# The opening of an attention and feed-forward kernel: softmax of the first batch in three groups of sets, x fetched ahead of the weights, three units opened together

## The chip, the cores and the metric

The kernel runs on one core of a Trainium2 chip. The metric is the device time of one execution in microseconds. The profile shows one execution on that core, with five instruction streams: PE (TensorE, with PEld for its weight loads), DVE (VectorE), ACT (ScalarE), POOL (GpSimd) and SP (SyncE, which here only issues DMAs).

## The reference

An attention block with inducing points is followed by a SwiGLU feed-forward block. There are 4 batches of 12416 tokens with 128 channels, 32 inducing points, and 1536 hidden channels.

```python
def mab(q, kv):
    s = scale * (q @ kv.transpose(0, 2, 1))
    s = s - s.max(-1, keepdims=True)
    a = np.exp(s)
    a /= a.sum(-1, keepdims=True) + 1e-09
    return a @ kv
h = mab(I, x)            # 32 inducing points attend to all tokens
x = mab(x, h)            # each token attends to the 32 rows of h
...
xn = x / rms * rms_g     # rms over the channels of a token
g = xn @ w_gate
silu = g * (1.0 / (1.0 + np.exp(-g)))
val = xn @ w_val
return (silu * val @ w_out).astype(np.float32)
```

The first softmax runs over all 12416 tokens of a batch, so no sum of it can be scaled before its last token has been seen. The weights of the feed-forward arrive as float64 and are turned to fp32 on the chip.

## The kernel before, in words

**Tiling.** A batch is cut into seven sets of tokens (`per`: five of 16 tiles of 128 tokens, one of 15, one of 2). A tile of x is turned to channels first by a PE transpose, `turn_x` (L313), four to a PSUM bank, and copied out by ACT (L316). `scores1` (L322, L326) multiplies a set with the inducing points, four groups of 32 rows side by side in one bank, and takes the maximum of each row as it copies the scores to SBUF. `max1`, `max2`, `max3` (L331 to L346) join the maxima of all sets: a reduction on DVE, a PE transpose, a reduction over the four groups and a scaling on DVE (`row`, `row4`), a PE matmul that turns the result back, and a copy of it to SBUF, the bias (`nbias`). `exp1_of` (L355) takes the exponential of one or two sets on ACT and sums its rows; `turn_e` (L364) transposes a set's exponentials in 32x32 blocks on DVE; `sum_h` (L378) multiplies them with the tokens on PE, with all seven sets in one PSUM bank. `fold_l` (L387, L389) adds up the row sums and takes the reciprocal, `divide` (L393) scales the sum, and `turn_h` (L398, L400) gives `hT`, the 32 rows of h with channels first.

From `hT` follow the second scores of set 0 (`scores2`, L322 and L424), the row maximum (L428, L432), the exponential (`exp2`, L439), and the steps of `seam`: a transpose, a product with the gram matrix of h for the rms (`square`, L499), row sums (L510), a power of -1/2 on POOL (`root`, L516), the scaling (`apply`, L520), a transpose and a split into an upper and a lower half (L524 to L533). `spread` (L555, L558) makes the first unit's moving operand out of these; `gather` (L545) makes those of later units by four DMAs.

**Weights.** Each weight matrix has three chunks (i, c): gate, value and output (i = 0, 1, 2), each for 512 hidden channels (c = 0, 1, 2). A chunk takes the steps `power`, `power_number`, `upper`, `upper_number`, `sign`, `lower` (L249 to L279): four on DVE, two on ACT (or on DVE where the code says so), the last product on POOL. Gate and value chunks are then multiplied with h (`stack_of` on PE and ACT, L467 and L468; `stack_low` on DVE, L472), since g = a (h w).

**Feed-forward units.** A unit is 512 tokens; a batch has 25, and each has 12 slots j, one for each 128 hidden channels. A slot is a gate matmul (L677), a silu on ACT (L685), a value matmul (L688), a product u on DVE (L694), and later the product with the output weights (L613), either plain in fp32 (two passes, 0.86 us) or as a three-part product of the kind of L633, L635 and L613, whose parts ACT, DVE and POOL prepare (L659 to L669). `acc` collects the unit's output.

**What sets the order.** No scheduler reorders: the code's order is the order on each engine's queue. The opening, up to the first slot, is written out by hand. From there a plan (`schedule`) puts the remaining weight steps, second scores and next batch's attention at given slots, and a rehearsal with costs by engine (`rehearse`, `decide`) settles which products are three-part ones and when each is issued. The slots of the first two units of batch 0 are sorted by weight chunk, so that the first eight slots need chunk 0 only. Calls of `warm` put matmuls with no use into PE's queue. [...] five in `ps_gv` (turns, scores, gate, value, stackings), two in `ps_acc`, one in `ps_u`.

**Queues.** All loads are issued on SP in the order: sets 0 to 3 of x, chunk (0,0), sets 4, 5 and 6 (four DMAs), then chunks (1,0), (2,0), (0,1) and (1,1); the two small loads (inducing points, gamma column) are on ACT's queue.

## Time and profile before

| | |
|---|---|
| time, median of 3 runs | 1623.82 us (1623.35 to 1623.96) |
| profiled run | 1623.49 us, span 1621.7 us |
| first turn of x on PE | 8.17 us |
| last pass of the first scores on DVE starts | 27.54 us |
| first exponential on ACT | 29.85 us |
| copy of hT on DVE | 39.45 us, 0.29 long |
| power of -1/2 on POOL | 48.29 us, 3.29 long |
| first gate matmul | 55.48 us |
| DMA share, 8 to 27 us | 0.93 |

A row of the timeline has the start, the duration, the engine, the line, the operation, the tile written, the tile read, their shapes, and in brackets how long the engine had been idle and what ended that. The chain of waits lists, in order of time, the pieces of work that the end depended on one after another. In the table of stretches each engine's column is its busy time within the stretch, and the last three columns are the granted PE clock, the share of the DMA engines that was busy, and GB/s.

### The profile page before, as it was taken

To read this page: it belongs to the slowest core of one execution; us is meant where nothing else is said; L and a number is where in the kernel's file an instruction comes from. 1 tells how busy PE (TensorE), PEld (TensorE's weight loads), DVE (VectorE), ACT (ScalarE), POOL (GpSimd) and SP (SyncE) were. 2 spreads that over 40 slices of the span, in tenths; PEclk is the share of its full clock that TensorE was granted. 3 is DMA by queue.
4 is the path that set the end of the run, shared out by engine and by line. 5 is a ranking of instruction groups with operands and counts; after the bars stand their busy time and mean duration, and the time that the engine had idled before them with its cause. 6 is when DMAs were issued, how large, how long until landed. Compare 5 with 4: busy or idle time off the path is not lost.

```text
span 1621.7 us, 25435 instructions
## 1 busy us (share of the span) xinstructions
PE 1604.3 (99%) x7085; PEld 1085.6 (67%) x7085; DVE 1444.6 (89%) x2504; ACT 1238.3 (76%) x2285; POOL 1217.7 (75%) x979
## 2 busy tenths in 40 slices
PE   8999999999999999999999999999999999999998
PEld 6546666756676666766677666676667777777776
DVE  4879988999899998899899998789989999999997
ACT  4567877767887778776778777877778888878886
POOL 1358885878588886688678888587858878878876
PEclk9999999999999999999999999999999999999999
DMA  7455624444353141634445323353221122111221
GB/s 262 91 72 85 112 43 97 88 97 69 60 94 59 36 95 29 133 76 81 69 67 83 55 54 68 63 125 79 46 38 29 31 39 40 35 35 36 40 38 26
DMA packets 389181, 112.52 MB, mean 69 GB/s; under 512 B 365072, under 2 KB 369712, under 8 KB 386480
## 3 DMA queue, kind: packets, MB, share of 16 engines
q1 hardware_dynamic: 388304, 110.82, 34.8%
q8 instruction: 56, 0.92, 0.3%
q14 instruction: 85, 0.70, 0.2%
q10 hardware_dynamic: 736, 0.08, 0.0%
HBM read 53.95 MB, written 27.00 MB: 50 GB/s over the span
## 4 chain that ended last, share of the span: by engine, by line
PE 94%; DVE 1%; ACT 1%; issue 1%; POOL 0%; DVEq 0%; ACTq 0%
PE acc L613 35%; PE gv L677 18%; PE gv L688 16%; PE u L635 10%; PE u L633 10%; PE gv L322 3%; PE gv L499 1%; PE gv L378 1%; DVE gv L694 1%; ACT silu L685 1%; PE gv L453 0%; DVE xn L660 0%; PE gv L467 0%; DVE o L621 0%; POOL xn L279 0%
## 5 line engine op out<-in xcount | busy, mean ns | idle before, releaser
L669 POOL TENSOR_TENSOR xn<-xn,xn 128x512 fp32r<-128x512 f32 (+2 forms) x705 | 870.9, 1255 | 268.6 <-DVE xn L660 156.8
L685 ACT ACTIVATE silu<-gv 128x512 f32<-128x512 f32 (+2 forms) x1186 | 689.7, 586 | 258.4 <-PE gv L677 231.8
L688 PE MATMUL gv<-a,sv 128*128 128x512 f32 (+2 forms) x1188 | 636.1, 536 | 0.8 <-ACT silu L685 0.8
L613 PE MATMUL acc<-u,wo 128*128 128x512 f32 (+1 forms) x990 | 490.8, 581 | 0.0
L677 PE MATMUL gv<-a,sg 128*128 128x512 f32 (+2 forms) x1188 | 486.7, 410 | 1.5 <-ACT silu L685 0.8
L694 DVE TENSOR_TENSOR u<-silu,gv 128x512 f32<-128x512 f32 (+2 forms) x621 | 407.7, 663 | 51.7 <-PE gv L688 32.3
L694 DVE TENSOR_TENSOR gv<-silu,gv 128x512 f32<-128x512 f32 (+2 forms) x565 | 376.0, 668 | 66.1 <-PE gv L688 49.0
L660 DVE SCALAR_TENSOR_TENSOR xn<-xn,gv 128x512 fp32r<-128x512 f32 (+2 forms) x566 | 371.3, 656 | 9.5 <-ACT xn L659 5.9
L659 ACT ACTIVATE xn<-gv 128x512 fp32r<-128x512 f32 (+2 forms) x566 | 330.4, 584 | 43.1 <-DVE gv L694 30.9
L677 PEld LDWEIGHTS gv<-a,sg 128*128 128x128 f32 x1188 | 223.8, 188 | 189.4 <-ACT silu L685 40.2
L688 PEld LDWEIGHTS gv<-a,sv 128*128 128x128 f32 x1188 | 223.6, 188 | 139.6 <-issue 46.3
L613 PE MATMUL acc<-xn,more 128*128 128x512 f32 (+2 forms) x705 | 273.6, 388 | 3.0 <-DVE o L621 2.6
L633 PE MATMUL u<-xn,xn 128*128 128x512 f32 (+2 forms) x705 | 272.4, 386 | 0.0
L613 PEld LDWEIGHTS acc<-u,wo 128*128 128x128 f32 x990 | 184.9, 188 | 46.7 <-issue 9.1
L664 POOL TENSOR_TENSOR xn<-u,xn 128x512 fp32r<-128x512 f32 (+2 forms) x139 | 178.6, 1285 | 41.6 <-ACT xn L663 41.6
L635 PE MATMUL u<-xn,xn 128*128 128x512 f32 (+2 forms) x414 | 160.1, 387 | 0.0
L613 PEld LDWEIGHTS acc<-xn,more 128*128 128x128 f32 x705 | 132.4, 188 | 33.5 <-POOL xn L669 5.7
L633 PEld LDWEIGHTS u<-xn,xn 128*128 128x128 f32 x705 | 132.6, 188 | 28.6 <-issue 5.5
L663 ACT ACTIVATE xn<-u 128x512 fp32r<-128x512 f32 (+2 forms) x139 | 87.4, 629 | 36.6 <-DVE u L694 32.4
L635 PE MATMUL u<-xn,more 128*128 128x512 f32 (+2 forms) x291 | 112.5, 387 | 0.0
L516 POOL TENSOR_TENSOR rs<-ms,mhalf 128x16 f32<-128x16 f32 (+2 forms) x28 | 75.9, 2709 | 18.1 <-DVE ms L511 17.1
L635 PEld LDWEIGHTS u<-xn,xn 128*128 128x128 f32 x414 | 77.7, 188 | 17.5 <-DVE gv L694 0.2
(151 smaller groups left out, 1096.9 us busy)
## 6 DMA issues: line engine op xcount, KB each, us to landing
out_dram<-o SPq DMA_DIRECT2D x320, 64.0 KB, 2.0
xT<-in_x_dram SPq DMA_DIRECT2D x60, 256.0 KB, 5.4
xn<-in_x_dram SPq DMA_DIRECT2D x60, 256.0 KB, 5.0
a<-hi SPq DMA_DIRECT2D x156, 64.0 KB, 2.0
a<-lo SPq DMA_DIRECT2D x156, 64.0 KB, 2.0
xn<-in_x_dram SPq DMA_DIRECT2D x5, 1024.0 KB, 10.6
xn<-w SPq DMA_DIRECT2D x18, 256.0 KB, 3.6
out_dram<-o SPq DMA_DIRECT2D x64, 60.0 KB, 2.0
```

What stands on the lines that cost most here:

```text
L613: nc.tensor.matmul(acc[:, 0:T], lhsT, rhs, start=st["left"] == NJ, stop=st["left"] == 1)
L633: nc.tensor.matmul(ups[:, 0:T], weight_of(0, j), hi, start=st["k"] == nk, stop=False)
L635: nc.tensor.matmul(ups[:, 0:T], weight_of(1, j), lo, start=False, stop=not st["k"])
L659: nc.scalar.activation(hi, v, AF.Copy, scale=(1.0 - 2.0 ** -13) * 2.0 ** -12)
L660: nc.vector.scalar_tensor_tensor(out=lo, in0=hi.bitcast(F32), scalar=-4096.0, in1=v, op0=ALU.mult, op1=ALU.add)
L663: nc.scalar.activation(d, v, AF.Copy, scale=1.0 - 2.0 ** -13)
L664: nc.gpsimd.tensor_tensor(out=lo, in0=v, in1=d.bitcast(F32), op=ALU.subtract)
L669: nc.gpsimd.tensor_tensor(out=d, in0=hi.bitcast(F32), in1=lo.bitcast(F32), op=ALU.subtract)
L677: nc.tensor.matmul(g[:, 0:T], sg[:, ts(j, P)], a[:, 0:T], start=True, stop=True)
L685: nc.scalar.activation(sl[:, 0:T], g[:, 0:T], AF.Silu)
L688: nc.tensor.matmul(v[:, 0:T], sv[:, ts(j, P)], a[:, 0:T], start=True, stop=True)
L694: nc.vector.tensor_tensor(out=t[:, 0:T], in0=sl[:, 0:T], in1=v[:, 0:T], op=ALU.mult)
```

## The change

It touches batch 0 only, apart from parameters that leave the other batches as they were.

- **Loads.** Set 6 of x comes first, as four DMAs on ACT's queue. Sets 0 to 5 follow on SP, with chunk (0,0) behind set 3, and set 5 in two DMAs (tiles 0 to 7, and the rest). The other four chunks follow behind set 5.
- **Softmax.** The sets are put in the groups 0 to 2, 3 to 4 and 5 to 6. Each group has a maximum of its own (`max1` to `max3` run three times), one exponential over its whole width and a PSUM bank of its own for its sum. `least` takes the smallest of the three biases, `shares` the exponentials of the differences, by which the row sums are weighted before `fold_l`; `divide` adds the three sums, each with its share and the common reciprocal, by one scaling and two fused multiply-adds.
- **Order of the opening.** Turns, scores, maxima, exponentials and sums of the groups are interleaved by hand. Two of the four copies of set 5 go to DVE. The calls of `warm` between the scores and the sums are gone. Chunk (0,0) is rounded between `max2` and `max3` of group 0 and behind that group's exponential; (1,0) around the end of the sums with its two number steps on ACT; (2,0) after the first exponential of the second softmax; (0,1) after `spread`.
- **First units.** Three units (`OPEN`) are opened together in place of two: the first 36 slots are sorted by chunk, so that the first 12 need chunk 0 only. The third unit's `acc` takes a bank of `ps_gv`. The plan puts chunks (1,1), (2,1), (2,2), (0,2), (1,2) at slots 2, 5, 8, 12, 16 and the stackings at 4, 8, 18, 22; the fourth unit's `gather` comes at slot j = 8 of the third.

```diff
+    GROUPS = (range(0, 3), range(3, 5), range(5, NS))
+    OPEN = 3
...
-                nc.sync.dma_start(out=t[ts(q, m), 0:n, :], in_=of(xrows, b, s)[q])
+                (nc.sync if b else nc.scalar).dma_start(out=t[ts(q, m), 0:n, :], in_=of(xrows, b, s)[q])
...
-            nc.sync.dma_start(out=t[:], in_=d)
+            for part in (slice(0, 8), slice(8, n)) if s == full - 1 else (slice(0, n),):
+                nc.sync.dma_start(out=t[:, part, :], in_=d[:, part, :])
...
-                nc.scalar.copy(out=dst, in_=src)
+                if k % 2 and s == full - 1:
+                    nc.vector.tensor_copy(out=dst, in_=src)
+                else:
+                    nc.scalar.copy(out=dst, in_=src)
...
+        def least():
+            st["least"] = small.tile([P, 1], F32, name="mx")
+            nc.vector.tensor_reduce(out=st["least"][:], in_=st["nb"][:], axis=AX.X, op=ALU.min)
+
+        def shares():
+
+            G, least = len(st["parts"]), st["least"]
+            share = st["share"] = small.tile([P, G], F32, name="rl")
+            nc.scalar.activation(share[:], st["nb"][:], AF.Exp, bias=least[:], scale=-1.0)
+            ls = st["ls"][:, 0:G]
+            nc.vector.tensor_tensor(out=ls, in0=ls, in1=share[:], op=ALU.mult)
+            nc.vector.reduce_sum(out=st["hl"][:, C:C + 1], in_=ls, axis=AX.X)
...
+                nc.vector.scalar_tensor_tensor(out=hn, in0=ps, scalar=share[:, g:g + 1], in1=hn, op0=ALU.mult, op1=ALU.add)
...
-        acc = ps_acc.tile([P, 512], F32, name="acc")
+        acc = bank() if not b and u == OPEN - 1 else ps_acc.tile([P, 512], F32, name="acc")
...
+    turn_x(0, *range(R))
+    f["scores1"](0)
+    turn_x(1, *range(R))
+    turn_x(2, *range(R))
+    f["scores1"](1)
+    f["scores1"](2)
+    f["max1"](0)
+    turn_x(3, *range(R))
+    f["max2"]()
+    parts(0, 0, nc.vector)
+    f["max3"](0)
+    f["exp1_of"](0, 3, 0)
+    f["scores1"](3)
+    join(0, 0)
+    f["turn_e"](0)
+    turn_x(4, *range(R))
+    f["turn_e"](1)
+    f["scores1"](4)
+    f["max1"](1)
+    turn_x(NS - 1, 0)
+    turn_x(5, 0, 1)
+    f["max2"]()
+    f["turn_e"](2)
+    f["scores1"](NS - 1)
+    f["max3"](1)
+    turn_x(5, 2, 3)
+    f["exp1_of"](3, 5, 1)
+    f["sum_h"](0)
+    f["scores1"](5)
+    f["max1"](2)
+    f["sum_h"](1)
+    f["turn_e"](3)
+    f["max2"]()
+    f["sum_h"](2)
+    f["turn_e"](4)
+    f["max3"](2)
+    f["exp1_of"](5, NS, 2)
+    f["least"]()
+    f["sum_h"](3)
+    f["sum_h"](4)
     one = weight[1, 0]
-    f["max1"]()
     one["power"]()
+    f["turn_e"](5)
+    f["turn_e"](6)
+    f["shares"]()
+    f["fold_l"]()
+    f["sum_h"](5)
+    f["sum_h"](6)
     one["upper"]()
+    one["power_number"]()
+    one["upper_number"]()
+    for g in range(len(GROUPS) - 1):
+        f["divide"](g)
+    one["sign"]()
+    f["divide"](len(GROUPS) - 1)
     f["turn_h"]()
...
-            for k, one in ((1, (2, 1)), (5, (0, 2)), (8, (1, 2)), (11, (2, 2))):
+            for k, one in ((2, (1, 1)), (5, (2, 1)), (8, (2, 2)), (12, (0, 2)), (16, (1, 2))):
...
-            for k, *one in ((2, 0, 1), (4, 1, 1), (11, 0, 2), (13, 1, 2)):
+            for k, *one in ((4, 0, 1), (8, 1, 1), (18, 0, 2), (22, 1, 2)):
...
-            order[:2 * NJ] = sorted(order[:2 * NJ], key=lambda one: (one[1] // R, one))
+            order[:OPEN * NJ] = sorted(order[:OPEN * NJ], key=lambda one: (one[1] // R, one))
```

## The prediction

> **What bounds the kernel now.** I read the page first: busy shares, then the chain that ended last.
>
> ```profile
> span 1621.7 us, 25435 instructions
> PE 1604.3 (99%) x7085; PEld 1085.6 (67%) x7085; DVE 1444.6 (89%) x2504; ACT 1238.3 (76%) x2285; POOL 1217.7 (75%) x979
> ...
> PE 94%; DVE 1%; ACT 1%; issue 1%; POOL 0%; DVEq 0%; ACTq 0%
> ```
>
> TensorE sets the end once the feed-forward units flow. The change leaves those units alone except the first three, so it can act only on the time before the first gate matmul, on the first 36 slots, and on the amount of TensorE work. The second view is the busy time by stretch (PE, PEld, DVE, ACT, POOL, clock, DMA share, GB/s).
>
> ```profile
> 8.00:27.00 19.00, 17.55 (x158) 12.24 (x158) 6.61 (x18) 12.30 (x25) 0.00 (x0) 1.00 0.93 369
> 27.00:40.00 13.00, 11.46 (x235) 9.48 (x237) 10.45 (x31) 5.06 (x10) 2.55 (x2) 1.00 0.41 124
> 40.00:55.50 15.50, 13.79 (x97) 10.70 (x89) 13.27 (x23) 7.10 (x14) 5.08 (x3) 1.00 0.14 41
> 55.50:62.40 6.90, 6.45 (x19) 3.44 (x20) 5.69 (x10) 4.28 (x8) 2.24 (x3) 1.00 0.60 163
> ```
>
> From 8 to 27 us TensorE (turns and scores of x) and the DMA are both nearly full and VectorE is idle two thirds of the time; from 27 to 40 VectorE is the full one. Of the opening's timeline these rows set prices:
>
> ```profile
> 23.70 0.42 DVE L249 TENSOR_SCALAR we<-sc 128x512 int32<-128x512 int32 x1
> 24.16 0.43 DVE L256 TENSOR_SCALAR we<-we 128x512 int32<-128x512 int32 x1
> 24.62 0.43 DVE L233 TENSOR_SCALAR we<-we 128x512 int32<-128x512 int32 x1
> 24.96 0.42 DVE L262 TENSOR_SCALAR o<-sc 128x512 int32<-128x512 int32 x1
> 25.41 0.43 DVE L233 TENSOR_SCALAR o<-o 128x512 f32<-128x512 int32 x1
> ...
> 29.65 0.16 DVE L346 COPY nbias<-gv 128x1 f32<-128x1 f32 x1 [0.20 <-PE gv L343]
> ...
> 29.85 0.72 ACT L355 ACTIVATE sc<-sc,nbias 128x512 f32<-128x512 f32 x1 [3.98 <-DVE nbias L346]
> 30.57 1.13 ACT L355 ACTIVATE sc<-sc,nbias 128x1024 f32<-128x1024 f32 x1
> ```
>
> The five instructions on weight chunk (0,0) hold VectorE 2.06 us (23.70 to 25.76). ScalarE waits 3.98 us for the bias of the one softmax.
>
> [...] L249 takes 0.80 at 27.88, while L279 runs on GpSimd, and 0.42 otherwise. [...] 0.69 for L326 from PSUM, 0.43 for the cast L532 from SBUF. [...] warm-up matmuls fill its waits; 20 cold ones at the start took 4.63 us, 16 warm ones at 29.55 took 2.05.
>
> **The change part by part.**
>
> *Loads.* Four issues for set 6 (0.31 to 0.42 each) leave SP and come on ScalarE ahead of its table load (1.68, 1.28 us), which then ends near 4.7; ScalarE's first copy starts at 8.80: hidden. In the built program chunk (0,0) waits in SP's queue for the gamma column (issue 1.21 plus 8.8 to landing: 10.0), with set 4 behind it; sets 2 and 3 keep the DMA full until 14.8, so nothing is lost. Set 4 landed at 18.5 (3.41+15.1), set 5 at 22.1 (4.50+17.6). The walk below wants them at 21.4 and 27.2, so the split of set 5 buys nothing either.
>
> *Groups.* I walk the new order with durations from before. Rates: a set's turns on PE 1.84, its copies on ACT 4x0.50, its scores 0.95, the scores pass on DVE 0.62 plus about 0.08, a transposed exponential 0.64, a set's sum 0.87. (Walked so, the scores of before end at 26.7; the last score matmuls of the trace end at 26.76.) Sets 0 to 2: scores of set 2 leave PE at 17.4, DVE has the group's maximum at 18.5, PE turns it behind set 3's turns at 19.3, row and row4 (0.27, 0.21) end at 20.15. Now the order puts the five (0,0) instructions ahead of the bias copy: +2.06, bias at 22.3. Behind that copy stand DVE's later passes, and ScalarE's exponential with all copies of set 4. The exponential over 1536 columns has no row; 0.72 and 1.13 give 0.41 per 512, so 1.54 (bounds 1.4 and 1.7). It ends at 23.9, set 4's copies at 25.9. PE, out of banks and inputs, stands from 23.2 to 26.0; set 4's scores end at 26.9. Group 1's maximum needs the DVE pass (27.8), a turn, one PSUM copy (0.6; bounds 0.43 and 0.72), row and row4: 29.4; bias 30.2. Set 5's second half is turned from 29.7, copied by 31.15, scored behind a sum from 31.3 to 32.2; its pass ends at 33.1, the third maximum at 33.3. Between 33.3 and 37.2 DVE does four transposes (0.64, two of them ahead of steps of the maximum), row, row4, bias (35.2), waits for the last exponential (36.06), two short transposes, and the new product and sum of the shares (0.15 each). Fold 0.42, reciprocal 0.17, upper 0.41, the scaling of shares 0.15, two of the three divides (0.35; the fused one bounded by 0.29 and 0.45): 39.2. Then the sign step, 0.6, stands ahead of the last divide: 40.15. Turn 0.49, copy 0.29: **hT at 41.0, against 39.74** (39.45+0.29). That is +1.3, bounds +0.5 and +2.1. The wins are real: in before 12.0 us pass from the last scores pass (27.76) to hT, in after 7.9. But the last scores come 5.3 later. The removed warm-ups (15) filled waits only: 0.
>
> *From hT to the first gate matmul* (55.48): scores, two-step maximum, exponential, gram, root (3.29 on GpSimd), apply, split, spread: 15.74 in before, each step waiting for the last. The order around it loses chunk (0,1) and half of (1,1) and gains (1,0)'s last step and all of (2,0). These fit where before had theirs, mostly under the root: 0.
>
> *First slots.* ScalarE now has two (0,1) steps (0.63, 0.60) between the spread's copy and the first silu: silu starts 0.65 later. From 55.48 to the gram matmul at 108.87 PE did 68 gate and value matmuls (0.2325), 28 products and 4 weight stackings (0.859), scores (5.24), one three-part product (0.70): 49.2 of 53.4, so 4.15 idle. After holds the same list but 29 products and no three-part one: 49.4. Of the idle time, 1.2 comes before the second stacking. With one stacking fewer ahead I get 1.05 including the late silu: -0.2. Some 0.5 lies at the wait for GpSimd's (1,2):
>
> ```profile
> 73.93 0.15 issue
> 74.08 1.35 POOL xn L279
> 75.43 0.04 issue
> 75.47 1.12 PE gv L467 x2
> ```
>
> (PE works until 75.0 meanwhile.) With chunks 1 and 2 needed at slots 12 and 24, not 8 and 16, it goes: -0.5. Against it, VectorE has a chunk and a half more to round (2.2 a chunk, 3.3 in all) in 36 slots; it was busy 24.0 of 31 from 78 to 109, so it holds. The third accumulator takes one of the five banks that gate, value, stacking and scores share, in slots 8 to 35: no row; between 0 and a wait of 0.15 in each of 28 slots, 4.2; I take +0.5.
>
> *Three-part products.* Two fewer in the built program (565 for 567 at 512 columns): 2x(0.859-0.70) = +0.3.
>
> **Sum:** +1.3-0.2-0.5+0.5+0.3 = +1.4 on a span of 1621.7, from a run of 1623.49; the three timed runs lie at 1623.35 to 1623.96. 1623.8+1.4 = **1625.2**.
>
> **Rivals.** *The clock drops.* PE's gap of 2.8 us ahead of set 4's scores [...] no warm-up fills it. For: nothing else is queued on PE; a GpSimd or exponential longer than priced widens it. Against: [...] the turns run at 0.112 each through 5.4 us at 11.9, so they keep the clock. [...] then scores (+0.95), 17 turns (+1.9) and a sum (+0.87) on the chain double: 3.7, of which I count 3.3 behind overlaps with VectorE: 1628.5, slower. *The lost bank decides.* 4.2 in place of 0.5: 1628.9; for it, a stacking bank is held about 3 us (PE, ACT cast, VectorE); against it, two slots' banks suffice on average. *The opening hides its steps and the ramp gains.* If VectorE is never the bound (bias and sign steps wait for nothing), hT comes at 39.0 or so (-2.0 to my walk), and three units remove 2.5 more of the 4.15 idle: 1620.6. For: less weight work per slot at first; against: VectorE's order is written out. *The change does not do what it says:* set 4 late behind the gamma wait. It needs 2.9 us of lateness; then the walk shifts by the rest; inside the ranges.
>
> **How the numbers follow.** Measurement tells 0.2% (3.2 us) from no change. Forecast 0.55 (own range 1622.8 to 1627.0), clock 0.15, bank 0.10, faster 0.20. The range reaches to the rivals: 1620.4 to 1628.7. Faster takes three quarters of the last rival, 0.15; slower most of the first two, 0.22; within 0.63.
>
> **What would show it.** First exponential near 22.4 and set 4's scores near 26 (right) or near 20.8 and 24 (faster rival); hT's copy near 40.7; first gate matmul near 56.8; turns at 0.23 each after 26 (clock); gate and value matmuls waiting for DVE or ACT in slots 8 to 35 (bank). Wrong altogether if the first gate matmul comes before 55.5.

## The result, and the profile after

The changed kernel takes **1635.93 us** (median of 4 runs, 1635.13 to 1636.19), the kernel before 1623.67 (4 runs, 1623.35 to 1623.96): a ratio of 1.0075, 95% interval 1.0057 to 1.0092. It is slower by 12.3 us where 1.4 were forecast, and lies outside the forecast range of 1620.4 to 1628.7. The page of after, its span, busy shares and the chain that ended last:

```profile
span 1633.2 us, 25381 instructions
...
PE 1606.0 (98%) x7059; PEld 1083.1 (66%) x7059; DVE 1447.8 (89%) x2512; ACT 1240.0 (76%) x2284; POOL 1218.5 (75%) x979
...
PE 93%; DVE 3%; ACT 2%; issue 1%; POOL 1%; DMA 0%; SPq 0%; DVEq 0%; POOLq 0%; ACTq 0%
```

TensorE still sets the end, with more of the chain on VectorE (3%, 1% in before) and ScalarE (2%, 1% in before). The busy time by stretch (PE, PEld, DVE, ACT, POOL, clock, DMA share, GB/s) tells where; the first two stretches are those shown of before, the third ends at the first gate matmul:

```profile
8.00:27.00 19.00, 14.98 (x120) 9.37 (x119) 8.09 (x22) 11.59 (x22) 1.27 (x1) 0.97 0.99 380
27.00:40.00 13.00, 11.47 (x235) 9.02 (x233) 8.49 (x31) 4.96 (x10) 0.00 (x0) 0.92 0.12 37
40.00:59.11 19.11, 15.19 (x98) 11.93 (x99) 14.57 (x25) 6.08 (x13) 5.95 (x4) 0.93 0.25 76
```

The clock column reads 0.97, 0.92 and 0.93 where before had 1.00 throughout: TensorE ran slower for part of each stretch. VectorE, the full engine from 27 to 40 in before (10.45 of 13), has 8.49.

**One offset has to be taken out first.** TensorE's first turn of x starts at 8.17 us in the run of before and at 7.22 in that of after, because the warm-up matmuls ahead of it come 0.21 us apart at first and 0.11 later, and the turn to the faster pace comes at 7.4 us in before and at 5.2 in after. So the same 33 matmuls, which start at 1.36 us in both, take 6.81 us and 5.86, and TensorE does not stand between them and the first turn. That is no part of the change. The opening of before ends (hT's copy) 31.57, 31.58, 31.57 and 31.58 us after its own first turn in all four runs here that have it, though the first turn itself lies anywhere from 7.11 to 8.17. So hT is counted from the first turn in what follows. With that, the loss falls into four stretches. "The gram matmul" is here the second one on TensorE (`square`, L499 in before and L530 in after); in every kernel of this document it comes behind 34 slots. A stretch ends with the end of hT's copy or the start of the matmul named:

| stretch | before | after | difference | forecast |
|---|---|---|---|---|
| first turn to hT | 31.57 | 34.47 | +2.9 | +1.3 |
| hT to the first gate matmul | 15.74 | 17.42 | +1.7 | 0 |
| first gate matmul to the gram matmul | 53.23 | 59.31 | +6.1 | −0.2 |
| gram matmul to the end | 1513.0 | 1514.8 | +1.8 | +0.3 |

They sum to +12.5; the two spans differ by 0.95 less, which is the earlier first turn. Half of the loss lies in these 34 slots. The same slots, split in three, in before (first fence) and in after (second):

```profile
55.48:74.00 18.52, 18.07 (x54) 9.97 (x55) 16.89 (x29) 12.07 (x22) 4.90 (x5) 1.00 0.76 152
74.00:90.00 16.00, 15.77 (x62) 7.02 (x61) 13.69 (x22) 10.60 (x19) 10.78 (x8) 1.00 0.55 79
90.00:108.71 18.71, 18.20 (x65) 8.51 (x64) 14.21 (x23) 13.11 (x20) 4.94 (x5) 1.00 0.41 60
```

```profile
59.11:78.00 18.89, 17.33 (x52) 9.13 (x51) 15.85 (x26) 11.64 (x22) 3.89 (x3) 0.98 0.65 132
78.00:99.00 21.00, 17.90 (x66) 7.40 (x65) 18.36 (x29) 12.27 (x23) 10.00 (x8) 1.00 0.34 64
99.00:118.42 19.42, 18.96 (x65) 8.82 (x64) 12.86 (x21) 13.30 (x20) 5.66 (x6) 1.00 0.43 67
```

The middle stretch carries it: TensorE stands 3.1 of 21.0 us, against 0.2 of 16.0. VectorE is busy 18.4 of 21.0 there, and 12.9 of 19.4 after it. What TensorE's matmuls waited for in these slots, in after (us in total, times, longest):

```profile
PE gv L708 <- DVE sg L503: 1.3, 1, 1.3
PE gv L644 <- DVE sv L503: 1.1, 1, 1.1
PE gv L330 <- ACT silu L716: 1.1, 1, 1.1
```

All three are waits for a bank: L503 is the last step of a stacking, which gives its bank back, and L716 is the silu that reads a gate matmul out of one. The second is the third unit's first product (`gv<-u,wo` at 76.01 us), whose sums move into a bank of `ps_gv`. Before has no wait above 0.5 us there. The question for the experiments was whether the bank is missing or the engines that give it back are late, and why.

### The profile page after: what moved, and what is told of

The parts are those of the page before. It is cut to its first block, busy times and chain, and to the rows that moved or that the text cites. A ratio compares the mean times of both kernels' runs of the same rounds, so it can differ in the third digit from the quotient of the medians.

```text
span 1633.2 us, 25381 instructions
## 1 busy us (share of the span) xinstructions
PE 1606.0 (98%) x7059; PEld 1083.1 (66%) x7059; DVE 1447.8 (89%) x2512; ACT 1240.0 (76%) x2284; POOL 1218.5 (75%) x979
## 4 chain that ended last, share of the span: by engine, by line
PE 93%; DVE 3%; ACT 2%; issue 1%; POOL 1%; DMA 0%; SPq 0%; DVEq 0%; POOLq 0%; ACTq 0%
PE acc L644 34%; PE gv L708 17%; PE gv L719 16%; PE u L666 10%; PE u L664 9%; PE gv L330 3%; PE gv L530 1%; PE gv L401 1%; ACT silu L716 1%; DVE gv L725 1%; ACT xT L324 0%; PE acc L186 0%; PE gv L318 0%; PE gv L484 0%; DVE u L725 0%
## 5 line engine op out<-in xcount | busy, mean ns | idle before, releaser
L700 POOL TENSOR_TENSOR xn<-xn,xn 128x512 fp32r<-128x512 f32 (+1 forms) x703 | 869.1, 1256 | 265.3 <-DVE xn L691 145.2
L716 ACT ACTIVATE silu<-gv 128x512 f32<-128x512 f32 (+2 forms) x1186 | 690.7, 587 | 255.9 <-PE gv L708 230.4
L644 PE MATMUL acc<-u,wo 128*128 128x512 f32 (+2 forms) x972 | 481.9, 580 | 0.0
L644 PE MATMUL acc<-xn,more 128*128 128x512 f32 (+1 forms) x702 | 272.5, 388 | 3.0 <-DVE o L652 2.7
L664 PE MATMUL u<-xn,xn 128*128 128x512 f32 (+1 forms) x703 | 271.6, 386 | 0.0
L695 POOL TENSOR_TENSOR xn<-u,xn 128x512 fp32r<-128x512 f32 (+1 forms) x141 | 181.5, 1287 | 42.5 <-ACT xn L694 42.5
L644 PEld LDWEIGHTS acc<-u,wo 128*128 128x128 f32 x972 | 181.4, 188 | 45.6 <-issue 8.4
L666 PE MATMUL u<-xn,xn 128*128 128x512 f32 (+2 forms) x412 | 159.3, 387 | 0.0
L694 ACT ACTIVATE xn<-u 128x512 fp32r<-128x512 f32 (+1 forms) x141 | 88.8, 630 | 37.7 <-DVE u L725 32.8
```

What stands on the lines that cost most here:

```text
L644: nc.tensor.matmul(acc[:, 0:T], lhsT, rhs, start=st["left"] == NJ, stop=st["left"] == 1)
L664: nc.tensor.matmul(ups[:, 0:T], weight_of(0, j), hi, start=st["k"] == nk, stop=False)
L666: nc.tensor.matmul(ups[:, 0:T], weight_of(1, j), lo, start=False, stop=not st["k"])
L694: nc.scalar.activation(d, v, AF.Copy, scale=1.0 - 2.0 ** -13)
L695: nc.gpsimd.tensor_tensor(out=lo, in0=v, in1=d.bitcast(F32), op=ALU.subtract)
L700: nc.gpsimd.tensor_tensor(out=d, in0=hi.bitcast(F32), in1=lo.bitcast(F32), op=ALU.subtract)
```

## The experiments

The table gives the median time of each run, its ratio to the kernel before on the same chip with the interval, and the four stretches of its own profile. Five runs whose first slots are those of after (after, x4, x9, y1, z1) give 59.24 to 59.43 for the third stretch, so in that column a difference of 0.2 says nothing.

| run | us | ratio, 95% | turn to hT | to gate | to gram | to end |
|---|---|---|---|---|---|---|
| x1_three_old_opening | 1624.89 | 1.0012 [1.0005, 1.0018] | 31.58 | 15.73 | 53.56 | 1514.6 |
| x2_two_new_opening | 1630.57 | 1.0045 [1.0030, 1.0060] | 34.06 | 17.41 | 56.39 | 1513.3 |
| x3_bank_back | 1632.42 | 1.0058 [1.0043, 1.0073] | 35.52 | 16.86 | 57.66 | 1514.2 |
| x4_warm | 1633.99 | 1.0066 [1.0049, 1.0083] | 34.03 | 17.43 | 59.39 | 1514.5 |
| x5_bank_held | 1624.68 | 1.0010 [1.0003, 1.0017] | 31.57 | 15.74 | 54.41 | 1513.6 |
| x6_fetch | 1633.22 | 1.0064 [1.0049, 1.0079] | 34.59 | 16.85 | 58.11 | 1514.9 |
| x7_lower | 1636.72 | 1.0082 [1.0067, 1.0098] | 35.52 | 15.81 | 60.97 | 1514.3 |
| x8_weights_early | 1632.28 | 1.0057 [1.0042, 1.0072] | 34.59 | 16.86 | 56.11 | 1515.0 |
| x9_warm_short | 1633.61 | 1.0064 [1.0049, 1.0079] | 32.97 | 16.86 | 59.43 | 1514.5 |
| y1_opening | 1633.92 | 1.0065 [1.0048, 1.0081] | 33.53 | 17.53 | 59.24 | 1514.6 |
| y2_two | 1627.93 | 1.0029 [1.0018, 1.0040] | 33.53 | 15.92 | 56.50 | 1513.3 |
| y3_three | 1626.45 | 1.0021 [1.0013, 1.0029] | 31.90 | 15.92 | 54.50 | 1514.0 |
| z4_bank_early | 1630.51 | 1.0044 [1.0029, 1.0059] | 32.97 | 16.86 | 54.79 | 1514.9 |
| z1_gather | 1635.33 | 1.0073 [1.0057, 1.0090] | 34.09 | 17.41 | 59.25 | 1514.5 |
| z2_three_bank_gather | 1623.14 | 1.0001 [0.9992, 1.0009] | 31.58 | 15.75 | 52.62 | 1514.1 |
| z3_opening | 1625.19 | 1.0013 [1.0006, 1.0020] | 31.32 | 15.92 | 54.50 | 1514.2 |

### Opening or first slots: each with the other's partner

**x1**, the kernel before with the three units alone:

```
+    OPEN = 3
-        acc = ps_acc.tile([P, 512], F32, name="acc")
+        acc = bank() if not b and u == OPEN - 1 else ps_acc.tile([P, 512], F32, name="acc")
-            order[:2 * NJ] = sorted(order[:2 * NJ],
+            order[:OPEN * NJ] = sorted(order[:OPEN * NJ],
...
```

> The kernel before, with its own opening and its own order of rounding and stacking, and only its first three units opened together, the third adding up in one of the five banks of gate and value. In the changed kernel the stretch from first gate matmul to gram matmul takes 59.3 us, in the kernel before 53.2. Bank theory (the third unit's sums hold a bank that gate, value, stacking and scores need): most of these 6 us come with the three units, so that stretch takes 57 to 60 us here, and the time is 1628 to 1631 us. Weight theory (the rounding that the new opening leaves to the first slots, and the late raw chunk, hold VectorE): the stretch takes 53 to 55 us, and the time is 1623.5 to 1625.5. Either way the first gate matmul stays at 55.5 us.

53.6 us, 1624.9: the weight theory's numbers. Three units and a lost bank by themselves cost 0.3 us in the first slots (and 1.6 behind the gram matmul).

**x2**, the changed kernel with two units:

```
-    OPEN = 3
+    OPEN = 2
-            for k, one in ((2, (1, 1)), (5, (2, 1)), (8, (2, 2)), (12, (0, 2)), (16, (1, 2))):
+            for k, one in ((1, (1, 1)), (3, (2, 1)), (6, (0, 2)), (9, (1, 2)), (12, (2, 2))):
-            for k, *one in ((4, 0, 1), (8, 1, 1), (18, 0, 2), (22, 1, 2)):
+            for k, *one in ((3, 0, 1), (6, 1, 1), (11, 0, 2), (14, 1, 2)):
...
```

> The changed kernel with its opening, but two units opened together, both adding up in their own banks; the weights that the opening leaves over are rounded in the order of the kernel before, each some slots later. The opening should give 3.6 us over the kernel before, as in the changed kernel (first gate matmul at 59.1 us). Bank theory: the stretch to the gram matmul takes 53 to 55 us, the time is 1627 to 1629. Weight theory: this stretch takes 57 to 60 us here too, the time is 1630 to 1634.

Between the two: 56.4 us, 1630.6. Without any lost bank the new opening still costs the first slots 3.2 us. It leaves one chunk more to them (22 rounding steps on VectorE where before has 18), and the four stackings wait 2.4 us in all for GpSimd's last step on their chunks, that of chunk (0,1) alone 1.53. So neither theory alone holds: the bank is cheap beside early weights, the late weights are dear even with all banks.

### The bank

**x3**, the changed kernel with the bank given back:

```
-        acc = bank() if not b and u == OPEN - 1 else ps_acc.tile([P, 512], F32, name="acc")
+        acc = ps_u.tile([P, 512], F32, name="u3") if not b and u == OPEN - 1 else ps_acc.tile([P, 512], F32, name="acc")
-            if (j >= NK or b == 0 and (u < OPEN - 1 or k < 26) or ...
+            if (j >= NK or b == 0 and (u < OPEN or k < 42) or ...
```

> The changed kernel with the sums of its third unit in the bank of the three-part products, which begin only at slot 42 instead of 26, so that gate, value, stacking and scores have five banks again; two three-part products fewer (+0.3 us). Bank theory: the waits of gate matmuls, products and scores for VectorE and ScalarE between 74 and 98 us (1.1 + 1.3 + 1.1 us and smaller ones) go, and the time falls by 3 to 5 us, to 1631 to 1633. Weight theory: the same waits stay, since VectorE and ScalarE are late by themselves, and the time stays within 1 us of 1636.

The stretch falls by 1.65 us, the ratio to 1.0058. (The profiled run, at 1633.8, is the slowest of this kernel's four, and its opening lost 1.05 us more than that of after; so the stretch is read here and not the time.) Of the three large waits, that of the products went from 1.1 to 0.3 (now of a value matmul) and that of the scores is gone (a gate matmul waits 0.6 for the silu), while the one at the stacking stayed:

```profile
PE gv L719 <- DVE sg L503: 1.3, 1, 1.3
```

So the bank is one cause of some 1.65 us, within the prediction's bounds of 0 to 4.2 but above its +0.5.

**x5**, the kernel before with one bank taken away in slots 8 to 35:

```
+            add(8, hold_bank)
+            add(35, free_bank)
...
+        nc.tensor.matmul(held[0][:, 0:P], ident[:], ident[:], start=True, stop=True)
...
+        nc.vector.tensor_copy(out=small.tile([P, 1], F32, name="mx")[:], in_=held.pop()[:, 0:1])
```

> The kernel before, with one of the five banks of gate and value taken at slot 8 by one more small matmul and given back at slot 35 by one more small VectorE copy; two three-part products fewer (+0.3 us). The two-unit ramp of before with four banks in these slots. If a bank is dear by itself: the stretch from first gate matmul to gram matmul grows by 2 to 4 us over 53.2, time 1626 to 1628. If it is dear only together with VectorE and ScalarE being late, as the three units with the old opening suggest (53.6 us with four banks): at most 0.7 us there, time 1623.5 to 1625.

54.4: +1.2 us, between the two expectations, and 1.0010 in time. But the stretch does not price the bank here: TensorE does 30 plain products in it where before does 28, at 0.86 us each. At the gate matmul of slot 60, where both kernels have done 53 products, x5 is 1.0 us behind before, 0.3 of it for two three-part products fewer. Beside early weights a bank is thus worth some 0.7 us by this run, and 0.9 by x1 against z2 below (53.6 and 52.6, with the same number of products); beside late ones it is 1.65.

### The weights

**x6**, chunks (0,2) and (2,2) exchanged:

```
-            for k, one in ((2, (1, 1)), (5, (2, 1)), (8, (2, 2)), (12, (0, 2)), (16, (1, 2))):
+            for k, one in ((2, (1, 1)), (5, (2, 1)), (8, (0, 2)), (12, (2, 2)), (16, (1, 2))):
```

> The changed kernel with chunks (2,2) and (0,2) changing places in the order of rounding: (0,2) from slot 8, (2,2) from slot 12. Its raw words, which SyncE fetches only after four loads of the next batch and the store of chunk (0,1), land at 74.7 us, 5.3 us after the issue at 69.4, and VectorE waits for them at slot 8. If this late landing matters: VectorE's wait at 73.6 (1.1 us) and the products' wait for the stack of VectorE at 76.0 (1.1 us) go, the stretch of 59.3 us falls to 57.5 to 58.5, the time to 1634 to 1635. If the slots 16 to 24 take it back (rounding beside the splitting of the out weights and the scores): less than 0.5 us.

58.1: 1.2 us gained, and the waits for the load and for L503 at 76 are gone. Not all of it need be the load: with chunk (0,2) four slots earlier, the wait for L503 at its stacking also fell, from 1.29 to 0.42 us. How chunk (2,2) came to be late shows in SyncE's queue (start, length of the issue), in before and in after:

```profile
58.69 0.53 SPq L221 DMA_DIRECT2D w<-xn  x1
59.31 0.40 SPq L209 DMA_DIRECT2D sg<-in_moe_w_out_dram  x1
59.81 3.87 SPq L146 DMA_DIRECT2D xT<-in_x_dram  x2
```

```profile
61.80 5.97 SPq L149 DMA_DIRECT2D xT<-in_x_dram  x4
67.87 1.45 SPq L224 DMA_DIRECT2D w<-xn  x1
69.42 0.39 SPq L212 DMA_DIRECT2D sg<-in_moe_w_out_dram  x1
```

The last step of chunk (0,1) also stores it and fetches the next raw chunk. In before it stood ahead of the next batch's loads; the change moved it into slot 1, behind four of them: 69.42 instead of 59.31. VectorE, whose order now wanted that chunk at slot 8 and not 11, then stood waiting for it:

```profile
74.73 0.50 DVE L252 TENSOR_SCALAR we<-sg 128x512 int32<-128x512 int32 x1 [1.13 <-DMA sg<-in_moe_w_out_dram]
75.27 0.69 DVE L503 TENSOR_TENSOR sv<-gv,sv 64x512 fp32r<-64x512 f32 x1
```

The stacking's L503, queued behind, gave its bank back at 75.96, and TensorE's product started at 76.01.

**x8**, all chunks and stackings early:

```
-            for k, one in ((2, (1, 1)), (5, (2, 1)), (8, (2, 2)), (12, (0, 2)), (16, (1, 2))):
+            for k, one in ((1, (1, 1)), (3, (2, 1)), (6, (0, 2)), (9, (1, 2)), (12, (2, 2))):
-            for k, *one in ((4, 0, 1), (8, 1, 1), (18, 0, 2), (22, 1, 2)):
+            for k, *one in ((4, 0, 1), (8, 1, 1), (11, 0, 2), (14, 1, 2)):
```

> The changed kernel with its three units, but the rounding of the remaining chunks at slots 1, 3, 6, 9 and 12 and the stackings at 4, 8, 11 and 14, instead of 2, 5, 8, 12, 16 and 4, 8, 18, 22. If the waits at 88 to 98 us (1.3 + 0.2 + 1.1 us) come from rounding and stacking of the last chunks lying beside the splitting of the out weights (slots 17 to 24) and the scores of the later sets (slots 18 to 30): they go, the stretch of 59.3 us falls to 56 to 57.5, time 1632.5 to 1634. If VectorE's total over 36 slots is what counts, or the missing bank alone, it stays at 58.5 to 60.

56.1: 3.2 us gained by order alone, with the same work, three units and four banks. No wait for L503 is left. The rounding of chunks (0,2) and (1,2) and their stackings had lain in slots 12 to 22, beside the splitting of the out weights (from slot 17) and the later sets' scores (from 18). How that pile reaches TensorE shows in after, ahead of the scores' wait of 1.11 us (L611 and L619 split the out weights, L282 is the last step of chunk (1,2)):

```profile
93.14 1.28 POOL L282 TENSOR_TENSOR xn<-o,we 128x512 f32<-128x512 f32 x1 [3.45 <-DVE o L280]
94.38 1.54 POOL L619 TENSOR_TENSOR more<-wo,xn 128x640 fp32r<-128x640 f32 x1
95.95 0.74 ACT L611 ACTIVATE more<-more 128x640 fp32r<-128x640 f32 x1 [2.05 <-POOL more L619]
96.59 0.58 ACT L716 ACTIVATE silu<-gv 128x512 f32<-128x512 f32 x1
97.22 1.07 PE L330 MATMUL gv<-xT,hT 128*32 128x512 f32 x8 [1.11 <-ACT silu L716]
```

The split waits on GpSimd behind the chunk, ScalarE waits for the split, and the silu that frees a bank stands behind it. GpSimd's last product on a chunk ends 35.3 us after the first gate matmul in after, 29.2 in x8 and 25.2 in before. x8 contains the exchange of x6, so 1.2 of its 3.2 us are that run's; the splitting and the scores were not moved by themselves.

**z4**, x3 and x8 together:

```
+        acc = ps_u.tile([P, 512], F32, name="u3") if not b and u == OPEN - 1 else ps_acc.tile([P, 512], F32, name="acc")
...
+            for k, one in ((1, (1, 1)), (3, (2, 1)), (6, (0, 2)), (9, (1, 2)), (12, (2, 2))):
...
```

> The changed kernel with both changes of the first slots at once: the third unit's sums in the bank of the three-part products, and the remaining chunks rounded at slots 1, 3, 6, 9 and 12 with stackings at 4, 8, 11 and 14. Alone the bank took the stretch from first gate matmul to gram matmul from 59.3 to 57.7 us, the early chunks took it to 56.1. If they are two causes that add: 54.0 to 55.0 us, and a time of 1630 to 1631.5. If they are two sides of the same waits (a bank given back late because VectorE is late): 55.5 to 56.5 us, 1631.5 to 1633.

54.8: 4.5 us gained, where 1.65 and 3.2 add up to 4.85. They are two causes. What is left over 53.2 lies mostly in stackings that wait for GpSimd's last step on their chunk:

```profile
PE gv L498 <- POOL xn L282: 1.4, 3, 0.6
```

Before has one such wait, of 0.2.

### The opening and the clock

**x4**, warm-up matmuls in both gaps:

```
+    warm(16)
     f["scores1"](4)
...
-    warm(26)
+    warm(42)
```

> The changed kernel with sixteen more 128x128 warm-up matmuls before the scores of set 4 and sixteen more in the run before the spread, nothing else. Clock theory (after an idle gap of 2.3 to 2.7 us TensorE runs at half speed for some us): the turns of sets 6 and 5 take 0.12 us each instead of 0.23, the spread's matmuls 0.5 instead of 0.8, hT's copy comes 0.3 to 1.2 us earlier than 41.4, the first gate matmul 0.9 to 1.8 us earlier than 59.1, and the time is 1634 to 1635. Rival (the slow matmuls lie beside VectorE's and ScalarE's work, which sets hT): only the spread gains, 0.6 us or less, and the time is above 1635.

Neither expectation came out: the ten turns ran warm (1.31 us, granted clock 1.00 from 26 to 30 us), but hT at 34.03 gained 0.4. I had put in too many: sixteen took 3.74 us, a gap of 2.42 was to be filled, so set 4's scores started 19.0 us after the first turn instead of 17.95, and the spread 0.55 later. **x9** has nine and eight more instead:

> The changed kernel with nine more warm-up matmuls (2.1 us at 0.234 each) before the scores of set 4 instead of sixteen, which took 3.74 us and put these scores off from 25.2 to 26.8, and eight more instead of sixteen before the spread, which they had put off from 56.8 to 57.9. Clock theory: the scores of set 4 start at 25.2 to 25.6 and take 1.07, the turns after them 0.12 each, hT's copy ends at 40.0 to 40.6 instead of 41.4 to 43.2, the spread's matmuls take 0.5, the first gate matmul comes at 56.9 to 57.5 instead of 59.1, and the time is 1632 to 1634. Rival (after 26 us VectorE and ScalarE set hT, whatever TensorE's clock): hT at 41.3 or later, first gate matmul at 58.2 or later.

hT comes 32.97 us after the first turn, 1.5 earlier than in after, and the first gate matmul at 57.54. TensorE in after, then in x9 (start, length, instructions):

```profile
25.17 1.49 PE L330 MATMUL gv<-xT,indT 128*32 128x512 f32 x8 [2.42 <-ACT xT L324]
26.59 2.40 PE L318 MATMUL gv<-ident,xn 128*128 128x128 f32 x10
```

```profile
23.07 2.17 PE L186 MATMUL acc<-ident 128*128 128x128 f32 x18
25.66 1.06 PE L330 MATMUL gv<-xT,indT 128*32 128x512 f32 x8 [0.42 <-ACT xT L324]
26.66 1.31 PE L318 MATMUL gv<-ident,xn 128*128 128x128 f32 x10
```

Ten turns take 2.40 us in one and 1.31 in the other; from 25 to 28 us the granted clock is 0.61 in after and 1.00 in x9. The clock theory holds: 1.5 us of the opening, in this run, are the lost clock. In the timed runs the ratio is 1.0064 against 1.0075, each within the other's interval, so the gain is not shown there.

**x7**, the last step of chunk (2,0) moved behind the split:

```
-    weight[2, 0]["lower"]()
     apply()
     turn_b()
     split()
+    weight[2, 0]["lower"]()
```

> The changed kernel with the last step of chunk (2,0) (one on VectorE, one on GpSimd) moved from ahead of the row factors to behind the split. If VectorE's step on the row factors took 1.75 us instead of 0.69 because GpSimd worked on that chunk beside it: it takes 0.69 here, the first gate matmul comes 0.8 to 1.1 us (a step of VectorE longer or shorter) earlier than 59.1, and the idle gap of TensorE ahead of the spread shrinks to 1.3 us or less, so that the spread's matmuls take 0.5 instead of 0.76 each and another 0.5 is won; the time is 1634 to 1635. If the length came from somewhere else (the broadcast operand), nothing moves.

The first half came true: from hT to the first gate matmul 15.81 instead of 17.42. The row factors' step in the chain of work of after and in the timeline of x7:

```profile
53.64 1.76 DVE sc L551
```

```profile
55.19 0.69 DVE L551 TENSOR_TENSOR sc<-sc,rs 128x512 f32<-128x512 f32 x1 [1.50 <-POOL rs L547]
```

In after GpSimd starts chunk (2,0)'s product at 53.58 (1.27 us), and VectorE's step on two operands in SBUF, begun at 53.64, takes 1.06 us longer than in x7, where no GpSimd instruction runs beside it. The time did not follow (1.0082): hT was at 35.52 in the profiled run, where the clock was lost (0.50 granted from 28 to 31 us), and the later step pushed the fetches on, so that VectorE's wait for chunk (2,2) grew from 1.13 to 1.90 us and the slots to 60.97.

**y1**, two shifts in VectorE's order:

```
-    parts(0, 0, nc.vector)
     f["max3"](0)
     f["exp1_of"](0, 3, 0)
     f["scores1"](3)
+    parts(0, 0, nc.vector)
...
-    one["sign"]()
     f["divide"](len(GROUPS) - 1)
     f["turn_h"]()
+    one["sign"]()
```

> The changed kernel with two shifts in its opening: the five VectorE steps of chunk (0,0) come behind the scores pass of set 3 instead of ahead of the first bias copy, and the sign step of chunk (1,0) behind hT's copy instead of ahead of the last divide. If VectorE's written order is what held the groups up: the first exponential starts at 19.3 to 19.8 instead of 21.5, set 4's scores at 23.0 to 23.6 instead of 25.2 with a gap of less than 1 us ahead of them [...], hT's copy ends at 38.3 to 39.6 instead of 41.7, the time falls by 2 to 3.5 us. If the arrival of sets 4 and 5 (18.5 and 22.1 us by the prediction) sets hT: it ends at 40.5 or later, and the time falls by less than 1.2.

The first exponential moved to 19.91 and set 4's scores to 23.56, as VectorE's order predicts. But hT gained only 0.94 (33.53), because VectorE came to the scores pass of set 4 later, and because the clock fell again at 29 us (0.50 granted from 29 to 32), behind gaps of only 0.99, 0.97 and 0.52.

### Everything taken away, and what is left

**y2** and **y3** join the two shifts, eight more warm-ups ahead of the spread, chunk (2,0)'s last step behind the split, chunk (0,1) whole before the first slots, and early chunks; y2 with two units, y3 with three and the bank of x3.

```
-    weight[2, 0]["lower"]()
+    parts(0, 1)
     apply()
     turn_b()
     split()
+    weight[2, 0]["lower"]()
     spread(0, 0)
-    parts(0, 1)
+    weight[0, 1]["sign"]()
     warm(3)
     gather(0, 1)
     gather(0, 2)
+    weight[0, 1]["lower"]()
...
-            for k, one in ((2, (1, 1)), (5, (2, 1)), (8, (2, 2)), (12, (0, 2)), (16, (1, 2))):
+            for k, one in ((0, (1, 1)), (3, (2, 1)), (6, (0, 2)), (9, (1, 2)), (12, (2, 2))):
...
```

> The two shifts of the opening, eight more warm-up matmuls ahead of the spread, chunk (2,0)'s last step behind the split, chunk (0,1) rounded whole before the first slots with its fetch of (2,2) ahead of the four loads of the next batch, and two units opened together with early chunks (slots 0, 3, 6, 9, 12). Every cost that the runs so far named is taken away: hT 38.3 to 39.6, 15.8 to the first gate matmul, 53.5 to 55 to the gram matmul, 1513.2 from there: 1621 to 1623.5 in the profile, 1622.5 to 1625 timed, within 0.1% of the kernel before. If something of the new opening is still unnamed, it is 1626 or more.

> The same opening with three units opened together, the third adding up in the bank of the three-part products, and the chunks at slots 0, 3, 6, 9 and 12 with stackings at 3, 7, 11 and 15. First gate matmul as in the run with two units. With five banks and early chunks the stretch to the gram matmul takes 53.0 to 54.5 us; the late gathering of the fourth unit's input (0.4 us of waiting for a DMA at 137.5 us in the changed kernel) and four fewer three-part products stay, so 1514.5 from there. 1 to 2 us slower than the run with two units: then the three units themselves are worth nothing even where their costs are gone. If they gain, it is faster than the run with two units.

y2 missed: it lies 2.9 us above the band, and its other case came true, a cost still unnamed. Its first slots take 56.5, with waits of the stackings for GpSimd of 1.45, 0.54, 0.47 and 0.22 us. Chunk (0,1) stood earlier in VectorE's order, but GpSimd ended it 3.07 us after the first gate matmul, against 0.8 in before, behind chunk (2,0). In y3 the case for a gain came true, 1.5 us ahead of y2: needing the second and third group's chunks four and eight slots later is worth something when the weights come late. (Its stackings also stand up to two slots later, which was not tried apart.) Its clock held (1.00 granted from 22 to 34 us) and hT came at 31.90.

**z3** is y3 with `join(0, 0)` moved behind the second bias, three warm-ups ahead of the second maximum's turn, and the fourth unit's gathering at slot 28:

```
-    join(0, 0)
     f["turn_e"](0)
...
     turn_x(5, 0, 1)
+    warm(3)
     f["max2"]()
...
     turn_x(5, 2, 3)
+    join(0, 0)
     f["exp1_of"](3, 5, 1)
```

> The run y3 with the last two VectorE steps of chunk (0,0) moved from ahead of set 4's scores pass to behind the second bias, three warm-up matmuls ahead of the second maximum's turn, and the gathering at slot 28. In y3 TensorE had set 4's scores ready at 25.7 us, and VectorE came to them at 26.95. If VectorE's order is what holds the groups up: hT's copy ends at 38.6 to 39.4 instead of 40.06, below the 39.74 of the kernel before, and the time is 1624.5 to 1625.7. If the three maxima one after the other set it (each a pass, a turn, two row steps and a bias copy): it ends at 39.7 or later, and groups cannot undercut the one softmax here.

hT at 31.32 after the first turn, 0.25 us *earlier* than the one softmax of before, and 1.0013 in time. (The 38.35 on the run's own clock looks better than that; 1.1 us of it is its early first turn.) So the groups work, but give a quarter of a microsecond, and hand over fewer weights: 54.5 in the first slots.

**z1**, the gathering alone:

```
-                if j == (6 if (b, u) == (0, R - 1) else 8 if not b and u == OPEN - 1 else 2) and (b or u > OPEN - 2) and (
-                        (b, u) in after):
-                    gather(*after[b, u])
+                if not b and u < OPEN:
+                    if (u, j) == (1, 8):
+                        gather(0, OPEN)
+                elif j == (6 if (b, u) == (0, R - 1) else 2) and (b, u) in after:
+                    gather(*after[b, u])
```

> The changed kernel with the fourth unit's input gathered at slot 28 instead of 32. If the wait of that unit's first gate matmul for the DMA (0.42 us at 137.5 us, after its DMAs stand behind loads of the next batch in SyncE's queue) is part of what is lost behind the gram matmul: it goes, and the stretch from the gram matmul to the end falls from 1514.8 to 1514.1 to 1514.5. If the three-part products and the slots after the exponentials are all of it: 1514.8 stays.

1514.5, in the expected band, but not for its reason: the wait for the load stays, 0.36 us at 137.35. It is the fifth unit's; in SyncE's queue that unit's gathering is issued at 133.03, right behind four stores. I had named the wrong unit.

**z2**, before's opening and weights with three units (x1), their bank (x3) and the gathering of z1:

```
+        acc = ps_u.tile([P, 512], F32, name="u3") if not b and u == OPEN - 1 else ps_acc.tile([P, 512], F32, name="acc")
...
+                    if (u, j) == (1, 8):
+                        gather(0, OPEN)
...
```

> The kernel before with its own opening and weight order, three units opened together, the third adding up in the bank of the three-part products, and the fourth's input gathered at slot 28: three units without the costs that the runs showed. With the bank in gate and value the stretch to the gram matmul took 53.6 us and the rest 1514.6. If three units are worth what a slower need for the chunks of the second and third group promises: 52.0 to 53.0 us, and 1513.5 to 1514.2 from there; time 1621.5 to 1623. If the wait for chunks was never the limit there: 53.2 or more, time 1623.5 to 1625.

1.0001 [0.9992, 1.0009]: no difference. The first slots take 52.6, 0.6 less than with two units, and 1.1 is given back behind the gram matmul. No version here beats the kernel before by a measurable amount.

Set side by side, the runs separate weights, bank and third unit (us from the first gate matmul to the gram matmul; x2 has its first two stackings one and two slots earlier than x8 and z4):

| weights in the slots | two units | three, bank lost | three, bank given back |
|---|---|---|---|
| as before | 53.2 | 53.6 (x1) | 52.6 (z2) |
| one chunk more, order of x8 | 56.4 (x2) | 56.1 (x8) | 54.8 (z4) |
| one chunk more, order of after | not run | 59.3 | 57.7 (x3) |

The bank costs 0.9 to 1.7 us. The third unit, its bank given back, gains 0.6 beside early weights and 1.6 beside late ones. The weights cost most in every column.

## Where the prediction was right and where it failed

*Groups, hT at 41.0.* Right. Counted from before's first turn (8.17), the walk had the first exponential at 22.4, set 4's scores at 26, hT's copy at 40.7. With after's first turn at 7.22 these are 21.45, 25.05 and 39.75; measured were 21.51, 25.17 and 41.40. The walk holds up to the clock, and with the clock held (x9, z4) hT comes 32.97 after the first turn: +1.40 over before, where +1.3 was forecast. The named cause, the five (0,0) steps ahead of the bias, is confirmed by y1; the sign step was moved in the same run and not tried alone.

*The clock, a rival at 0.15.* It happened. The prediction took a gap of 2.8 us for one that probably keeps the clock. That was its estimate: the longest gap in before between the first turn and the first gate matmul is 1.26 us (at 53.66, granted clock 1.00). In after the gap was 2.42, and it still cost 1.5 us before hT and 0.6 more at the spread, where a second gap, of 2.33 us, left its two matmuls at 0.76 and 0.80 instead of 0.47 and 0.51. The price of 3.3 us was too high: against the 32.97 of the kept clock, five runs with this opening lost 1.1 to 1.6 us (after, x2, x6, x8, z1) and two lost 2.55 (x3, x7). From 31 to 34 us the granted clock is still 0.58 and 0.54 in these two, and 1.00 in the five.

*From hT to the first gate matmul, 0.* Failed: "these fit where before had theirs, mostly under the root". The moved step of chunk (2,0) fits under nothing: its product begins when the root ends on GpSimd, beside the VectorE step that it slows. +1.06, and +0.6 for the spread's clock. The prediction had seen L249 take 0.80 us beside a GpSimd product and 0.42 otherwise, and did not ask what the moved step would run beside.

*First slots, −0.2 in all.* **This is the step that failed**, by 6.3 us, more than half of the miss. "VectorE has a chunk and a half more to round ... it was busy 24.0 of 31 from 78 to 109, so it holds" took an average over 31 us. VectorE's total did fit (47.1 us of 59.3 are busy); its order did not. The plan puts two chunks and two stackings into slots that already carried the splitting of the out weights and the scores, and VectorE, ScalarE and GpSimd each reach the step that frees a bank late: 3.2 us (x8). The amount was off too: the plan leaves one chunk more to these slots, not one and a half, yet VectorE's rounding there takes 15.7 us for 11.2, +4.5 where 3.3 were priced. Steps ran longer than their price, as L252 at 85.41 with 1.18 us instead of 0.42 while GpSimd worked on a chunk (85.03 to 86.31). The lost bank, taken at +0.5, costs 1.65 on top (x3), and the two nearly add (z4). About 1.6 remains, mostly waits for GpSimd's chunks. The −0.5 for chunk (1,2)'s wait was given back by such a wait for chunk (1,1), 0.44 us at 70.89.

*Loads: hidden.* Right for x. Missed for weights: the last step of chunk (0,1) carries a fetch, and was moved past four loads on SyncE. 1.2 us of the 3.2 go with x6, in part for another reason (see there).

*Three-part products, +0.3.* The count is right; behind the gram matmul the loss is 1.8. All runs with three units take 1514.0 to 1515.0 there, those with two units and all banks 1513.0 to 1513.3. In after it has come about by slot 60: the gate matmul there is 7.8 us behind that of before, the last one 7.9. Between slots 32 and 60 after has two plain products for two three-part ones (0.3) and two waits that before has not, 0.49 for VectorE's u and 0.42 for a load, 1.2 of 1.7 in all; the rest is open. The faster rival fell: with its costs taken away, the ramp of three units wins 0.6 in the slots and nothing in time (z2).

## What to carry to other kernels

When a change postpones work into a stage that is "not full", lay it over the other queues of that stage slot by slot; the average busy share says nothing about the engine that frees a buffer, and a lost buffer and a late releaser add up. Of a step that moves, follow each thing that it issues: here a fetch behind four loads, and a GpSimd product beside a two-operand step of VectorE on the path, which took 1.75 us for 0.69. Before two profiles are compared to a microsecond, subtract the start of their first dependent instruction. Fill a TensorE gap with just as many warm-ups as fit: nine in a gap of 2.42 us won 1.5, sixteen won 0.4, since they delayed the next work by 1.1.

## What the runs showed of the hardware

- **The same gap loses the clock in one run and not in another; what tells them apart was not shown.** In eight runs with the same opening up to there and no warm-ups added, TensorE waited 2.42 or 2.43 us before set 4's scores. Seven lost the clock (0.50 to 0.82 granted from 25 to 28 us; the next ten turns took 2.1 to 2.4 us); z4 kept it (1.00; 1.31 us). Eight runs waited 2.31 to 2.33 us ahead of the spread; after, x2, z1 and y1 lost it there (its second matmul took 0.79 or 0.80 us), x3, x6, x8 and z4 did not (0.50 or 0.51). y1 and y2 lost it at 29 us (0.50 granted from 30 to 32) behind gaps of 0.97 and 0.52; y3, the same instructions but starting 1 us later, kept it (1.00) and reached hT 1.63 us sooner. So the length of one gap does not decide in these runs: gaps of 2.31 to 2.43 us lost the clock eleven times and kept it five times, and two runs lost it behind shorter ones.
- **The start of the opening varies, what follows repeats.** The 33 warm-up matmuls from 1.36 us on take 5.48 us (x6) to 6.87 us (z4). In the four runs with the opening of before, hT comes 31.57 or 31.58 us after the first turn, while that turn varies by 1.1 us.
- **A VectorE step with two SBUF inputs beside a GpSimd product** took 1.75 us (after, y1), and 0.69 without it (before, x7).
